# A fixed order for VectorE's first block, and one batch's sums on TensorE, in an attention and feed-forward kernel

## The chip, the cores and the metric

The kernel runs on one core of a Trainium2 chip. The metric is the device time of one execution in microseconds; the time before is the median of three runs.

## What is computed

Eight batches of 576 positions go through attention with eight heads of 64, whose keys and values are first averaged over groups of eight positions (72 per batch remain). The result, 4608 tokens of width 512, goes through two feed-forward layers. Reference, cut to what matters:

```python
k_p = k.reshape(B, H, Sp, 8, D).mean(axis=3)          # Sp = 72
v_p = v.reshape(B, H, Sp, 8, D).mean(axis=3)
scores = q @ k_p.transpose(0, 1, 3, 2) / sqrt(D)
attn = softmax(scores)                                 # max subtracted, 1e-9 added to the sum
x = (attn @ v_p)  -> rows of 512                       # 4608 x 512
h = x @ w_in;  g = h * sigmoid(1.702 * h);  x = g @ w_out        # 512 -> 2048 -> 512
out = ((x @ w_a) * (x @ w_b)) @ w_out2                 # 512 -> 1536 -> 512
```

The weights arrive as 64-bit floats.

## The kernel before

**Tiles and passes.** Tokens go in nine blocks of 512, each made of four *units* of 128. Each feed-forward layer is done in two passes over the nine blocks, with a part of its hidden columns each (six and ten tiles of 128 columns in layer 1, four and eight in layer 2). A *step* is one hidden tile f of one block: `emit_h` (L325) makes h = x w_in for 128 hidden columns with twelve matmuls into PSUM, then g; `emit_y` (L342) adds g's product with w_out into four accumulators, twelve matmuls more. Every operand is a pair of a high part in a rounded format and a low part that holds the rest, so each product is three matmuls (`mm3`, L110): high by high (L111), high by low (L112), low by high (L113). `split` (L68) makes such a pair: ScalarE rounds (L70), VectorE subtracts (L71).

**Weights.** A weight tile arrives as pairs of 32-bit words. `convert` (L87) makes high and low part out of them: four steps on VectorE (L92, L93, L94, L98), the rounding on ScalarE (L101), four more on VectorE (L103, L104, L107, L108). Each hidden tile has two such conversions, e = 0 for w_in and e = 1 for w_out.

**Attention.** `sum_k` (L165) adds groups of eight positions of the keys, half a batch's heads at a time, in one VectorE reduction (L170), and ScalarE copies the result in two pieces into `kbd` (L172, L173), laid out so that one matmul makes the scores of two heads. `sum_v` (L181) does the same for the values (L184). Per unit: `stage_b1` (L186), twice for four heads each, makes the scores on TensorE (L200), takes their maximum on VectorE (L207), scales and negates it (L208), and lets ScalarE take the exponentials with their sum (L211); `stage_b2` (L220) normalises on VectorE in three dependent steps (L223, L224, L225); `stage_c` (L227) transposes on TensorE (L233) and copies (L234); `stage_d` (L237) multiplies by the summed values (L246) and splits the result into x, high and low.

**What sets the order.** The program's text is followed by a list scheduler: it takes instructions by their place in the text and by modelled times, and interleaves independent work on each engine. What comes out is fixed: each engine works through its own queue in order and waits in front of an instruction until its operands are there. The exception before is `tc.issue_after(...)`, which holds later conversions behind a named instruction (`spread_late`, L421). At the start the text loads keys, queries, values and weights of batches 0 and 1 through SP's queue (L508 to L525), where each transfer waits for the one eight places ahead of it; does units 0 to 3 with the first weight tiles in between (L526 to L541); and then runs the steps, in each of which the text has the next step's `emit_h`, the extra work that `todo` holds (conversions, sums and attention of later units), and this step's `emit_y` (L552 to L562).

Of the kernel before, what the change touches and what calls it, by code (L numbers as in the profile page):

```python
# [24 lines left out]
def tile_kernel(ctx, tc, q, k, v, w_in, w_out, w_a, w_b, w_o2, out):  # L25
# [39 lines left out]
    def f32(ap):  # L65
        return ap.bitcast(F32)

    def split(hi, lo, src):  # L68

        nc.scalar.copy(out=hi, in_=src)  # L70
        nc.vector.tensor_tensor(out=lo, in0=src, in1=f32(hi), op=ALU.subtract)  # L71


    words = {
# [12 lines left out]
    def convert(units):  # L87


        for raw, t, hi, lo in units:  # L90
            low, high = raw[:, :, 0], raw[:, :, 1]
            nc.vector.tensor_scalar(out=t, in0=high, scalar1=0x7FFFFFFF, scalar2=None, op0=ALU.bitwise_and)  # L92
# [5 lines left out]
            nc.vector.scalar_tensor_tensor(  # L98
                out=t, in0=high, scalar=0xC0000000, in1=t, op0=ALU.bitwise_and, op1=ALU.bitwise_or
            )  # L100
            nc.scalar.copy(out=hi, in_=f32(t))  # L101

            nc.vector.tensor_scalar(out=high, in0=t, scalar1=0xFF800000, scalar2=None, op0=ALU.bitwise_and)  # L103
            nc.vector.scalar_tensor_tensor(  # L104
                out=f32(low), in0=low, scalar=2.0 ** -52, in1=f32(high), op0=ALU.mult, op1=ALU.mult
            )
            nc.vector.tensor_tensor(out=f32(t), in0=f32(t), in1=f32(hi), op=ALU.subtract)  # L107
            nc.vector.tensor_tensor(out=lo, in0=f32(t), in1=f32(low), op=ALU.add)  # L108

    def mm3(o, whi, wlo, xhi, xlo, first, last):  # L110
        nc.tensor.matmul(out=o, lhsT=whi, rhs=xhi, start=first, stop=False)  # L111
# [50 lines left out]
        nc.sync.dma_start(out=raw, in_=k[b, :, 2 * half:2 * half + 2, :])  # L162
        kraw_t[b, half] = raw

    def sum_k(b, half):  # L165
# [4 lines left out]
        nc.vector.tensor_reduce(out=ks, in_=raw, op=ALU.add, axis=AX.X)  # L170
        cs = slice(2 * half, 2 * half + 2)
        nc.scalar.copy(out=kbd[b % 2][0:D, cs, 0:SP], in_=ks[0:D])  # L172
        nc.scalar.copy(out=kbd[b % 2][D:P, cs, SP:2 * SP], in_=ks[D:P])  # L173
# [7 lines left out]
    def sum_v(b, h, n):  # L181
        if h == 0:
            vs_t[b] = ap_.tile([SP, H, D], F32, tag="vs", name="vs", bufs=2)
        nc.vector.tensor_reduce(out=vs_t[b][:, h:h + n, :], in_=vraw_t.pop((b, h)), op=ALU.add, axis=AX.X)  # L184

    def stage_b1(u, half):  # L186
        qT = q_t[u]
        if half == 0:
            at_t[u] = (
                ap_.tile([P, H, SP], F32, tag="at", name="at", bufs=2),  # L190
                ap_.tile([P, H], F32, tag="mx", name="mx", bufs=2),
                ap_.tile([P, H], F32, tag="sm", name="sm", bufs=2),
            )
        a, mx, sm = at_t[u]
        scale = 1.0 / (POOL * D ** 0.5)
# [12 lines left out]
        nc.vector.tensor_scalar_mul(mx[:, hs], mx[:, hs], -scale)  # L208
        for c in range(H // 2):
            h = half * (H // 2) + c  # L210
            nc.scalar.activation(  # L211
                out=a[:, h, :], in_=sc[:, c, :], func=AF.Exp, scale=scale, bias=mx[:, h:h + 1],
                accum_out=sm[:, h:h + 1],
            )
        if half == 1:
            q_t.pop(u)
            if UB <= u + 2 < NU:
                load_q(u + 2)

# [38 lines left out]
    def op(f, *a):  # L258
        return lambda: f(*a)
# [30 lines left out]
    def as_words(t):  # L290
        return t.rearrange("p (f w) -> p f w", w=2)
# [6 lines left out]
            return columns("a", f), columns("b", f)  # L298
        return rows("o2", 2 * f), rows("o2", 2 * f + 1)

    def load_w(key, raw=None):
        if raw is None:
            raw = wp.tile([P, 2, 1024], U32, tag="w", name="raw")
        raw_t[key] = raw
        for e, src in enumerate(sources(key)):
            nc.sync.dma_start(out=as_words(raw[:, e]), in_=src)

    nconv = [0]

    def make_w(key, e):  # L310

        if e == 0:
            w_t[key] = wp.tile([P, 4, 512], F32R, tag="w", name="w")
        w = w_t[key]
        t = tmps[nconv[0] % len(tmps)]
        nconv[0] += 1
        convert([(as_words(raw_t[key][:, e]), t, w[:, e, :], w[:, 2 + e, :])])
        if e == 1:
            raw_t.pop(key)


    anchors = {}
# [2 lines left out]
    def emit_h(i, j, f):  # L325
        xhi, xlo = x_t[i, j]
        w = w_t[1, f]
        hps = ps.tile([P, N], F32, tag="ps", name="h")
        for kk in range(KD):
            cs = slice(kk * P, (kk + 1) * P)  # L330
            mm3(hps, w[:, 0, cs], w[:, 2, cs], xhi[:, kk, :], xlo[:, kk, :], kk == 0, kk == KD - 1)

        g = gp.tile([P, N], F32, tag="g", name="g", bufs=1)
        ghi = gp.tile([P, N], F32R, tag="ghi", name="ghi")
        glo = gp.tile([P, N], F32R, tag="glo", name="glo")
        nc.scalar.activation(out=g, in_=hps, func=AF.Tanh, scale=0.5 * 1.702)  # L336
        made = nc.vector.scalar_tensor_tensor(out=g, in0=g, scalar=1.0, in1=hps, op0=ALU.add, op1=ALU.mult)  # L337
        split(ghi, glo, g)
        anchors[i, j, f] = made.ins
        g_t[i, j, f] = (ghi, glo)  # L340
# [187 lines left out]
    for t, ops in enumerate(slots):  # L528
        if t == 2:
            for half in range(2):  # L530
                sum_v(0, half * H // 2, H // 2)
        for o in ops:
            o()
        if t == 0:
            make_w((1, 0), 0)
        if t == 2:
            make_w((1, 0), 1)
            load_w((1, 3))
        if t == 3:
            make_w((1, 1), 0)  # L540
    make_w((1, 1), 1)  # L541

    for n in range(FA - 2):
        ops = [op(make_w, (1, n + 2), e) for e in range(2)]
        if n + 4 < FA:
            ops.append(op(load_w, (1, n + 4)))
        if n == 0:
            ops += [op(sum_k, 1, 0), op(sum_k, 1, 1), op(sum_v, 1, 0, H // 2), op(sum_v, 1, H // 2, H // 2)]
        todo[n] = ops + todo[n]

    first(steps[0])
    for n, s in enumerate(steps):  # L552
        if n == place[1, 0, FA]:
            at.close()
            p2 = ctx.enter_context(tc.tile_pool(name="p2", bufs=2))
            rooms += [p2.tile([P, 2, 1024], U32, name=f"room{e}", bufs=1) for e in range(2)]
            tmps[:] = [p2.tile([P, 512], U32, name=f"tmp{e}", bufs=1) for e in range(2)]
        if n + 1 < len(steps):
            first(steps[n + 1])
        for o in todo[n]:  # L560
            o()
        second(s)  # L562
# [47 lines left out]
```

## Time and profile before

| | |
|---|---|
| median of three runs | 1853.39 us (1850.32 to 1856.36) |
| the profiled execution | 1854.09 us |
| its span, first to last instruction | 1852.3 us |
| TensorE busy | 1803.3 us, 97% of the span, 8592 matmul records |
| VectorE busy | 847.4 us, 46% |
| ScalarE busy | 543.8 us, 29% |
| mean granted clock of TensorE | 0.987 |

In the profile PE is TensorE, DVE VectorE, ACT ScalarE and SP the engine that issues the transfers. The shares are means over the whole span and hide that its start is another regime than the rest; the windows below show the busy time of each engine by stretch. The granted clock is the share of TensorE's full 2.4 GHz that it ran at; 0.50 is its lower level of 1.2 GHz. A float32 matmul of the program (scores, transposed products) shows as two records, a transpose or a matmul of the rounded format as one. Consecutive rows of VectorE overlap a little: an instruction that does not depend on the one ahead starts before that one's end.

### The profile page before, as it was taken

How to read it: one execution, taken by the hardware profiler on the slowest of the kernel's cores; microseconds unless marked ns; L12 is line 12 of the kernel's file. 1: busy time of each engine (PE TensorE's matmuls, PEld its weight loads, DVE VectorE, ACT ScalarE, POOL GpSimd, SP SyncE). 2: the span in 40 equal slices, each digit the busy share in tenths (PEclk: the TensorE clock that was granted, in tenths of full speed). 3: DMA queues.
4: the chain of work that ended last, by engine and by line, in shares of the span. 5: the costliest groups of instructions: out<-in, count | busy, mean ns of one | idle time of the engine just before them, and what ended most of it. 6: DMA issues, size and time to landing. Idle time of an engine off the chain costs nothing.

```text
span 1852.3 us, 21637 instructions
## 1 busy us (share of the span) xinstructions
PE 1803.3 (97%) x8592; PEld 1485.8 (80%) x8592; DVE 847.4 (46%) x1524; ACT 543.8 (29%) x1361; POOL 1.7 (0%) x8
## 2 busy tenths in 40 slices
PE   3889999999999999999999999999999999999998
PEld 2668888888888888888888888888888888888887
DVE  7967677756644444445444444456212221221222
ACT  3556555554232222223222222222111111111111
POOL 0000000000000000000000000000000000000000
PEclk8789999999999999999999999999999999999999
DMA  8454444324433222333224433432201210220200
GB/s 259 163 180 150 165 148 157 127 86 163 178 114 110 96 100 93 126 125 134 100 82 152 159 137 105 168 114 91 91 28 64 91 61 30 91 91 8 84 24 23
DMA packets 58613, 206.92 MB, mean 112 GB/s; under 512 B 6576, under 2 KB 6576, under 8 KB 46704
## 3 DMA queue, kind: packets, MB, share of 16 engines
q1 hardware_dynamic: 58512, 205.55, 31.4%
q8 instruction: 67, 1.10, 0.2%
q14 instruction: 34, 0.28, 0.1%
HBM read 139.46 MB, written 66.06 MB: 111 GB/s over the span
## 4 chain that ended last, share of the span: by engine, by line
PE 94%; DMA 3%; DVE 2%; ACT 0%; issue 0%; SPq 0%; DVEq 0%; ACTq 0%
PE ab L112 11%; PE ab L111 11%; PE ab L113 11%; PE acc L112 7%; PE acc L111 7%; PE acc L113 7%; PE h L111 7%; PE h L112 7%; PE h L113 7%; PE acc L376 5%; PE acc L375 5%; PE acc L377 5%; PE sc L200 2%; PE px L246 2%; PE pt L233 2%; DMA kraw<-in_k_dram 1%
## 5 line engine op out<-in xcount | busy, mean ns | idle before, releaser
L111 PE MATMUL ab<-xhi,w 128*128 128x512 f32 x864 | 336.1, 389 | 0.0
L112 PE MATMUL ab<-xlo,w 128*128 128x512 f32 x864 | 336.1, 389 | 0.0
L113 PE MATMUL ab<-xhi,w 128*128 128x512 f32 x864 | 336.1, 389 | 0.0
L363 DVE TENSOR_TENSOR c<-c,ab 128x512 f32<-128x512 f32 x108 | 74.2, 687 | 530.3 <-PE ab L113 530.3
L112 PE MATMUL acc<-glo,w 128*128 128x512 f32 x576 | 229.0, 398 | 5.0 <-DVE glo L71 5.0
L113 PE MATMUL acc<-ghi,w 128*128 128x512 f32 x576 | 227.6, 395 | 0.0
L111 PE MATMUL h<-xhi,w 128*128 128x512 f32 x576 | 226.2, 394 | 0.7 <-ACT xhi L70 0.7
L112 PE MATMUL h<-xlo,w 128*128 128x512 f32 x576 | 224.9, 390 | 0.0
L113 PE MATMUL h<-xhi,w 128*128 128x512 f32 x576 | 224.6, 390 | 0.0
L337 DVE SCALAR_TENSOR_TENSOR g<-g,h 128x512 f32<-128x512 f32 x144 | 98.5, 684 | 228.4 <-ACT g L336 228.0
L111 PE MATMUL acc<-ghi,w 128*128 128x512 f32 x576 | 187.6, 401 | 3.9 <-ACT ghi L70 3.8
L111 PEld LDWEIGHTS ab<-xhi,w 128*128 128x128 f32 x864 | 162.2, 188 | 33.8
L113 PEld LDWEIGHTS ab<-xhi,w 128*128 128x128 f32 x864 | 162.2, 188 | 33.7
L112 PEld LDWEIGHTS ab<-xlo,w 128*128 128x128 f32 x864 | 162.2, 188 | 33.6
L336 ACT ACTIVATE g<-h 128x512 f32<-128x512 f32 x144 | 86.1, 598 | 322.5 <-PE h L113 309.8
L376 PE MATMUL acc<-w,chi 128*128 128x512 f32 x432 | 168.1, 389 | 0.0
L375 PE MATMUL acc<-w,chi 128*128 128x512 f32 x432 | 168.1, 389 | 0.0
L362 ACT COPY c<-ab 128x512 f32<-128x512 f32 x108 | 63.4, 587 | 356.3 <-PE ab L113 356.3
L377 PE MATMUL acc<-w,clo 128*128 128x512 f32 x432 | 167.6, 389 | 0.0
L70 ACT CAST chi<-c 128x512 fp32r<-128x512 f32 x108 | 66.9, 620 | 288.4 <-DVE c L363 288.4
L112 PEld LDWEIGHTS acc<-glo,w 128*128 128x128 f32 x576 | 109.3, 190 | 28.4 <-DVE glo L71 6.2
L111 PEld LDWEIGHTS acc<-ghi,w 128*128 128x128 f32 x576 | 107.4, 190 | 26.5 <-ACT ghi L70 5.1
(61 smaller groups left out, 2070.8 us busy)
## 6 DMA issues: line engine op xcount, KB each, us to landing
part<-ys SPq DMA_DIRECT2D x72, 256.0 KB
part<-part SPq DMA_DIRECT2D x18, 1024.0 KB
xhi<-yd SPq DMA_DIRECT2D x18, 1024.0 KB
xlo<-yd SPq DMA_DIRECT2D x18, 1024.0 KB
xd<-xhi SPq DMA_DIRECT2D x9, 1024.0 KB
xd<-xlo SPq DMA_DIRECT2D x9, 1024.0 KB
xhi<-xd SPq DMA_DIRECT2D x9, 1024.0 KB
xlo<-xd SPq DMA_DIRECT2D x9, 1024.0 KB
```

Source lines behind the costliest of these rows:

```text
L70: nc.scalar.copy(out=hi, in_=src)
L111: nc.tensor.matmul(out=o, lhsT=whi, rhs=xhi, start=first, stop=False)
L112: nc.tensor.matmul(out=o, lhsT=whi, rhs=xlo, start=False, stop=False)
L113: nc.tensor.matmul(out=o, lhsT=wlo, rhs=xhi, start=False, stop=last)
L200: nc.tensor.matmul(out=sc[o:o + n, 2 * c:2 * c + 2, :].rearrange("p h k -> p (h k)"), lhsT=qT[:, pair, o:o + n], rhs=kbd[b % 2][:, pair, : ...
L336: nc.scalar.activation(out=g, in_=hps, func=AF.Tanh, scale=0.5 * 1.702)
L337: made = nc.vector.scalar_tensor_tensor(out=g, in0=g, scalar=1.0, in1=hps, op0=ALU.add, op1=ALU.mult)
L362: nc.scalar.copy(out=cc, in_=pab[0])
L363: made = nc.vector.tensor_tensor(out=cc, in0=cc, in1=pab[1], op=ALU.mult)
L375: nc.tensor.matmul(out=o, lhsT=chi[:, cs], rhs=whi, start=first, stop=False)
L376: nc.tensor.matmul(out=o, lhsT=chi[:, cs], rhs=wlo, start=False, stop=False)
L377: nc.tensor.matmul(out=o, lhsT=clo[:, cs], rhs=whi, start=False, stop=last)
```

## The change

1. *A fixed order for VectorE in the first block.* `vec` notes the newest VectorE instruction of a group, and `in_order` issues each next group behind it, so that the groups stand in VectorE's queue in the order of the text. The work before the first step, and that beside the six steps of the first block, is written out in this way. A conversion is cut in two parts (`part` 0 and 1), `emit_h` gives back its two VectorE steps as pieces, and `filler` puts conversion parts and attention pieces between them.
2. *Batch 1's sums on TensorE.* `sum_k_pe` and `sum_v_pe` add the eight positions by eight matmuls with the identity into one PSUM tile, each reading every eighth word of the raw keys or values; ScalarE copies the sums out. Batches 0 and 2 to 7 keep the reductions.
3. *Scaling.* The keys are scaled when they are copied into `kbd`, the maximum is negated by the reduction that takes it, and the multiplication (L208) is gone.
4. *The first conversion step* of the six tiles of the first pass is an absolute value on ScalarE instead of a mask on VectorE.
5. *Loads.* Part e = 1 of the first weight tile is loaded behind the values of batch 0 and the second unit's queries.

```diff
+    def in_order(*ops):
+        for o in ops:
+            if newest[0] is None:
+                o()
+            else:
+                with tc.issue_after(newest[0]):
+                    o()
...
+            if first_on_act:
+                nc.scalar.activation(out=f32(t), in_=f32(high), func=AF.Abs)
+            else:
+                nc.vector.tensor_scalar(out=t, in0=high, scalar1=0x7FFFFFFF, scalar2=None, op0=ALU.bitwise_and)
...
+    def to_kbd(b, half, ks):
+        cs = slice(2 * half, 2 * half + 2)
+        nc.scalar.mul(out=kbd[b % 2][0:D, cs, 0:SP], in_=ks[0:D], mul=scale)
+        nc.scalar.mul(out=kbd[b % 2][D:P, cs, SP:2 * SP], in_=ks[D:P], mul=scale)
...
+    def sum_k_pe(b, half):
+        ks = ps.tile([P, 2, SP], F32, tag="ps", name="ksp")
+        raw = kraw_t.pop((b, half)).rearrange("p c (s r) -> p c s r", r=POOL)
+        for r in range(POOL):
+            nc.tensor.matmul(out=ks, lhsT=ident, rhs=raw[:, :, :, r], start=r == 0, stop=r == POOL - 1)
+        to_kbd(b, half, ks)
...
+    def sum_v_pe(b, h, n):
...
+        vp = ps.tile([SP, n, D], F32, tag="ps", name="vsp")
+        for r in range(POOL):
+            nc.tensor.matmul(
+                out=vp, lhsT=ident[:SP, :SP], rhs=raw[:, :, :, r], start=r == 0, stop=r == POOL - 1
+            )
+        nc.scalar.copy(out=vs_t[b][:, h:h + n, :], in_=vp)
...
-        nc.vector.tensor_reduce(out=mx[:, hs], in_=sc, op=ALU.max, axis=AX.X)
-        nc.vector.tensor_scalar_mul(mx[:, hs], mx[:, hs], -scale)
+        vec(nc.vector.tensor_reduce(out=mx[:, hs], in_=sc, op=ALU.max, axis=AX.X, negate=True))
...
+    c0, c1 = make_parts((1, 0)), make_parts((1, 1))
+    in_order(op(sum_k, 0, 0), op(sum_k, 0, 1), b1(0)[0], c0[0], b1(0)[1], b1(1)[0], c0[1], b1(1)[1])
+    in_order(op(sum_v, 0, 0, half_v), b2(0), op(sum_v, 0, half_v, half_v), b2(1), *b1(2))
+    in_order(c0[2], cd(0), b1(3)[0], c0[3], cd(1), b1(3)[1], b2(2), c1[0], b2(3), c1[1], cd(2), c1[2], cd(3), c1[3])
...
+    hs[0] = emit_h(*steps[0])
     for half in range(2):
-        sum_k(0, half)
...
+        sum_k_pe(1, half)
+    in_order(hs[0][0])
+    filler(1)
+    in_order(hs[0][1])
+    for n in range(1, FA):
+        hs[n] = emit_h(*steps[n])
+        second(steps[n - 1])
+        if n == 1:
+            sum_v_pe(1, 0, half_v)
+            sum_v_pe(1, half_v, half_v)
+        filler(2)
+        in_order(hs[n][0])
+        filler(1)
+        in_order(hs[n][1])
+        filler(1)
+    in_order(*ahead_)
```

VectorE's queue before, from the first g (L337) on: `tmp_126` and `tmp_127` are two conversions in work, `raw_298` and `raw_469` their tiles, `mx` the maxima, `ks` a key sum.

```order
L337 SCALAR_TENSOR_TENSOR g_423<-g_423,h_410 128x512
L103 TENSOR_SCALAR raw_298<-tmp_127 128x512
L92 TENSOR_SCALAR tmp_126<-raw_469 128x512
L207 TENSOR_REDUCE mx_484<-sc_497 128x4
L170 TENSOR_REDUCE ks_979<-kraw_892 128x144
L207 TENSOR_REDUCE mx_513<-sc_515 128x4
L104 SCALAR_TENSOR_TENSOR raw_298<-raw_298 128x512
L107 TENSOR_TENSOR tmp_127<-tmp_127,w_593 128x512
L93 TENSOR_SCALAR tmp_126<-tmp_126 128x512
L207 TENSOR_REDUCE mx_513<-sc_527 128x4
L71 TENSOR_TENSOR glo_425<-g_423,ghi_424 128x512
```

The same place of the changed kernel, whose first g is L395, g's low half L400, the first conversion half L111 to L116, the second L122 to L127, and a unit's normalisation L266 to L268:

```order
L111 TENSOR_SCALAR tmp_126<-tmp_126 128x512
L112 TENSOR_SCALAR tmp_126<-tmp_126 128x512
L116 SCALAR_TENSOR_TENSOR tmp_126<-raw_151,tmp_126 128x512
L251 TENSOR_REDUCE mx_453<-sc_455 128x4
L251 TENSOR_REDUCE mx_453<-sc_465 128x4
L400 TENSOR_TENSOR glo_417<-g_415,ghi_416 128x512
L122 TENSOR_SCALAR raw_151<-tmp_126 128x512
L123 SCALAR_TENSOR_TENSOR raw_151<-raw_151 128x512
L126 TENSOR_TENSOR tmp_126<-tmp_126,w_446 128x512
L127 TENSOR_TENSOR w_446<-tmp_126,raw_151 128x512
L251 TENSOR_REDUCE mx_539<-sc_541 128x4
L266 TENSOR_SCALAR sm_454<-sm_454 128x8
```

Two conversions were interleaved step by step with sums and maxima; now the steps of one half follow each other, and the maxima of units 4 and 5 stand between the halves.

TensorE's queue before, at the first activation (`h_410`; `h_430` is the second, `sc` scores of unit 4, `kbd0` and `kbd1` the keys of batches 0 and 1):

```order
L111 MATMUL h_410<-xhi_252,w_187 128x512
L111 MATMUL h_430<-xhi_252,w_351 128x512
L200 MATMUL sc_486<-kbd0_122,q_274 64x144
L200 MATMUL sc_486<-kbd1_123,q_274 64x144
L200 MATMUL sc_486<-kbd0_122,q_274 64x144
L200 MATMUL sc_486<-kbd1_123,q_274 64x144
L112 MATMUL h_410<-xlo_253,w_187 128x512
```

The same place of the changed kernel, with the first activation `h_402` and the key sums `ksp` by halves of the heads:

```order
L130 MATMUL h_402<-xhi_265,w_180 128x512
L205 MATMUL ksp_419<-kvraw_147,ident_78 128x144 x8
L205 MATMUL ksp_430<-kvraw_149,ident_78 128x144 x2
L131 MATMUL h_402<-xlo_266,w_180 128x512
L132 MATMUL h_402<-xhi_265,w_180 128x512
L130 MATMUL h_402<-xhi_265,w_180 128x512
```

Ten of the sixteen key-sum matmuls now stand inside the first activation; the other six follow it, then unit 4's scores.

## Rows read from the trace of the kernel before

**Rows 1.** Busy time of each engine (instructions) by windows; granted clock; DMA share, GB/s.

```profile
0.00:30.00 30.00, 8.62 (x36) 6.95 (x36) 21.30 (x39) 11.20 (x45) 1.73 (x8) 1.00 0.96 296
30.00:60.00 30.00, 17.39 (x102) 12.81 (x102) 25.86 (x52) 13.19 (x46) 0.00 (x0) 0.57 0.52 161
60.00:100.00 40.00, 32.94 (x184) 25.09 (x180) 38.50 (x83) 20.50 (x80) 0.00 (x0) 0.84 0.57 192
100.00:120.00 20.00, 17.79 (x87) 14.07 (x88) 11.91 (x24) 10.95 (x45) 0.00 (x0) 0.76 0.31 90
120.00:1852.00 1732.00, 1726.59 (x8191) 1426.84 (x8189) 749.84 (x1329) 487.94 (x1147) 0.00 (x0) 1.00 0.30 106
```

**Rows 2.** Who waited for whom, 0 to 130 us: total us, times, longest.

```profile
PE pt L233 <- DVE at L225: 19.7, 4, 8.5
...
PE acc L112 <- DVE glo L71: 5.0, 2, 3.3
...
DVE ks L170 <- ACT kbd L173: 2.0, 1, 2.0
```

**Rows 3.** VectorE's timeline, a later conversion and a normalisation: start us, us.

```profile
1028.28 0.69 DVE L98 SCALAR_TENSOR_TENSOR tmp<-room,tmp 128x512 uint32<-128x512 uint32 x1
1029.01 0.43 DVE L103 TENSOR_SCALAR room<-tmp 128x512 uint32<-128x512 uint32 x1
1029.47 0.69 DVE L104 SCALAR_TENSOR_TENSOR room<-room 128x512 f32<-128x512 uint32 x1
1030.08 0.68 DVE L107 TENSOR_TENSOR tmp<-tmp,w 128x512 f32<-128x512 f32 x1
1030.80 0.69 DVE L108 TENSOR_TENSOR w<-tmp,room 128x512 fp32r<-128x512 f32 x1
...
105.75 0.17 DVE L223 TENSOR_SCALAR sm<-sm 128x8 f32<-128x8 f32 x1 [0.79 <-ACT at L211]
105.96 0.20 DVE L224 RECIPROCAL sm<-sm 128x8 f32<-128x8 f32 x1
106.20 0.76 DVE L225 TENSOR_TENSOR at<-at,sm 128x576 f32<-128x576 f32 x1
```

**Rows 4.** VectorE's timeline where conversions are interleaved, 64 to 66 us.

```profile
64.63 0.41 DVE L94 TENSOR_SCALAR tmp<-tmp 128x512 uint32<-128x512 uint32 x1
64.97 0.68 DVE L104 SCALAR_TENSOR_TENSOR raw<-raw 128x512 f32<-128x512 uint32 x1
65.57 0.68 DVE L107 TENSOR_TENSOR tmp<-tmp,w 128x512 f32<-128x512 f32 x1
```

**Rows 5.** Groups by line, 0 to 130 us: busy us, mean ns, idle before.

```profile
L184 DVE TENSOR_REDUCE vs<-kvraw 72x256 f32<-72x2048 f32 x4 | 9.1, 2280 | 3.3 <-DMA kvraw<-in_v_dram 3.2
L207 DVE TENSOR_REDUCE mx<-sc 128x4 f32<-128x288 f32 x20 | 8.9, 446 | 4.4 <-PE sc L200 4.3
...
L170 DVE TENSOR_REDUCE ks<-kvraw 128x144 f32<-128x1152 f32 x4 | 5.4, 1350 | 7.7 <-DMA kvraw<-in_k_dram 5.7 <-ACT kbd L173 2.0
...
L184 DVE TENSOR_REDUCE vs<-vraw 72x128 f32<-72x1024 f32 x4 | 4.8, 1211 | 2.5 <-DMA vraw<-in_v_dram 2.5
...
L208 DVE TENSOR_SCALAR mx<-mx 128x4 f32<-128x4 f32 x20 | 3.0, 156 | 0.0
...
L101 ACT CAST w<-tmp 128x512 fp32r<-128x512 f32 x12 | 7.5, 626 | 21.1 <-DVE tmp L98 21.1
```

**Rows 6.** TensorE's timeline: scores at both clocks, end of the second block's first activation.

```profile
39.41 1.17 PE L200 MATMUL sc<-kbd,qs 128*128 128x144 f32 x4
...
84.43 0.65 PE L200 MATMUL sc<-kbd,q 128*128 128x144 f32 x4
84.83 0.49 PE L112 MATMUL acc<-glo,w 128*128 128x512 f32 x1
...
128.93 0.39 PE L112 MATMUL h<-xlo,w 128*128 128x512 f32 x1
129.16 0.39 PE L113 MATMUL h<-xhi,w 128*128 128x512 f32 x1
```

More of the change, by code (lines that the diff above doesn't have):

```diff
@@ L85, in rows, with convert @@
         return words[name][f * P:(f + 1) * P, :, :]
[L87 to L92, printed above, removed]
+    def convert(raw, t, hi, lo, part, first_on_act=False):
+        low, high = raw[:, :, 0], raw[:, :, 1]
+        if part == 0:
+            if first_on_act:
+                nc.scalar.activation(out=f32(t), in_=f32(high), func=AF.Abs)
+            else:
+                nc.vector.tensor_scalar(out=t, in0=high, scalar1=0x7FFFFFFF, scalar2=None, op0=ALU.bitwise_and)
             nc.vector.tensor_scalar(out=f32(t), in0=f32(t), scalar1=LOW, scalar2=HIGH, op0=ALU.max, op1=ALU.min)
@@ L96, in convert @@
             )
-            nc.vector.scalar_tensor_tensor(
+            vec(nc.vector.scalar_tensor_tensor(
                 out=t, in0=high, scalar=0xC0000000, in1=t, op0=ALU.bitwise_and, op1=ALU.bitwise_or
-            )
+            ))
             nc.scalar.copy(out=hi, in_=f32(t))
[L103 to L108, printed above, removed]
+            return
+        nc.vector.tensor_scalar(out=high, in0=t, scalar1=0xFF800000, scalar2=None, op0=ALU.bitwise_and)
+        nc.vector.scalar_tensor_tensor(
+            out=f32(low), in0=low, scalar=2.0 ** -52, in1=f32(high), op0=ALU.mult, op1=ALU.mult
+        )
+        nc.vector.tensor_tensor(out=f32(t), in0=f32(t), in1=f32(hi), op=ALU.subtract)
+        vec(nc.vector.tensor_tensor(out=lo, in0=f32(t), in1=f32(low), op=ALU.add))
     def mm3(o, whi, wlo, xhi, xlo, first, last):
@@ L169, in sum_k @@
         raw = kraw_t.pop((b, half)).rearrange("p c (s r) -> p c s r", r=POOL)
[L170 to L173, printed above, removed]
+        vec(nc.vector.tensor_reduce(out=ks, in_=raw, op=ALU.add, axis=AX.X))
+        to_kbd(b, half, ks)
[4 more added lines that the diff above has]
+            nc.tensor.matmul(out=ks, lhsT=ident, rhs=raw[:, :, :, r], start=r == 0, stop=r == POOL - 1)
+        to_kbd(b, half, ks)
     def load_v(b, h, n, raw=None):
@@ L211, in stage_b1 @@
             nc.scalar.activation(
-                out=a[:, h, :], in_=sc[:, c, :], func=AF.Exp, scale=scale, bias=mx[:, h:h + 1],
+                out=a[:, h, :], in_=sc[:, c, :], func=AF.Exp, bias=mx[:, h:h + 1],
                 accum_out=sm[:, h:h + 1],
@@ L299, in sources, with load_w @@
         return rows("o2", 2 * f), rows("o2", 2 * f + 1)
-    def load_w(key, raw=None):
+    def load_w(key, raw=None, parts=(0, 1)):
         if raw is None:
@@ L305, in load_w @@
         for e, src in enumerate(sources(key)):
+            if e not in parts:
+                continue
             nc.sync.dma_start(out=as_words(raw[:, e]), in_=src)
@@ L316, in make_w, with make_parts, one @@
         nconv[0] += 1
-        convert([(as_words(raw_t[key][:, e]), t, w[:, e, :], w[:, 2 + e, :])])
+        for part in range(2):
+            convert(as_words(raw_t[key][:, e]), t, w[:, e, :], w[:, 2 + e, :], part)
         if e == 1:
             raw_t.pop(key)
+    def make_parts(key):
+        def one(e, part):
+            if (e, part) == (0, 0):
+                w_t[key] = wp.tile([P, 4, 512], F32R, tag="w", name="w")
+            w = w_t[key]
+            convert(as_words(raw_t[key][:, e]), tmps[e], w[:, e, :], w[:, 2 + e, :], part, True)
+        return [op(one, e, part) for e in range(2) for part in range(2)]
     anchors = {}
@@ L336, in emit_h, with rest @@
         nc.scalar.activation(out=g, in_=hps, func=AF.Tanh, scale=0.5 * 1.702)
[L337 to L340, printed above, removed]
+        def rest():
+            made = vec(nc.vector.scalar_tensor_tensor(out=g, in0=g, scalar=1.0, in1=hps, op0=ALU.add, op1=ALU.mult))
+            nc.scalar.copy(out=ghi, in_=g)
+            anchors[i, j, f] = made.ins
+            g_t[i, j, f] = (ghi, glo)
+        return rest, lambda: vec(nc.vector.tensor_tensor(out=glo, in0=g, in1=f32(ghi), op=ALU.subtract))
     def emit_y(f, gs, ya, first, last):
@@ L433, in first @@
         i, j, f = s
-        (emit_h if passes[i][0] == 1 else emit_ab)(i, j, f)
+        if passes[i][0] == 1:
+            for o in emit_h(i, j, f):
+                o()
+        else:
+            emit_ab(i, j, f)
     sums = {}
@@ L445, in second @@
             finish(i, j, sums.pop((i, j)))
-    for j in range(1, NB):
-        ts = range(UB if j == 1 else UB * j + 2, UB * (j + 1) + 2)
-        spread([o for t in ts for o in later[t]], max(0, place[0, j - 1, 0] - 1), place[0, j, 0] - 1)
+    for j in range(2, NB):
+        ts = range(UB * j + 2, UB * (j + 1) + 2)
+        spread([o for t in ts for o in later[t]], place[0, j - 1, 0] - 1, place[0, j, 0] - 1)
     for i in range(1, 4):
@@ L513, in tile_kernel @@
     next(kv0)
-    load_w((1, 0))
-    next(kv0)
+    load_w((1, 0), parts=(0,))
     load_q(1, qs[:, 1])
     next(kv0)
+    next(kv0)
+    load_w((1, 0), raw_t[1, 0], (1,))
     load_q(2, qs[:, 2])
+    load_q(3, qs[:, 3])
     load_w((1, 1))
-    load_q(3, qs[:, 3])
     next(kv1)
@@ L525, in tile_kernel @@
     next(kv1)
-    for half in range(2):
-        sum_k(0, half)
[L528 to L549, printed above, removed]
@@ L551, in tile_kernel, with b1, b2, cd @@
-    first(steps[0])
+    load_w((1, 3))
+    half_v = H // 2
+    def b1(u):
+        return [op(stage_b1, u, half) for half in range(2)]
+    def b2(u):
+        return op(stage_b2, u)
+    def cd(u):
+        return lambda: (stage_c(u), stage_d(u))
+    c0, c1 = make_parts((1, 0)), make_parts((1, 1))
+    in_order(op(sum_k, 0, 0), op(sum_k, 0, 1), b1(0)[0], c0[0], b1(0)[1], b1(1)[0], c0[1], b1(1)[1])
+    in_order(op(sum_v, 0, 0, half_v), b2(0), op(sum_v, 0, half_v, half_v), b2(1), *b1(2))
+    in_order(c0[2], cd(0), b1(3)[0], c0[3], cd(1), b1(3)[1], b2(2), c1[0], b2(3), c1[1], cd(2), c1[2], cd(3), c1[3])
@@ new lines, in tile_kernel, with filler @@
+    ahead_ = [o for t in range(UB, 2 * UB + 2) for o in later[t]]
+    parts = [o for f in range(2, FA) for o in make_parts((1, f))]
+    per = -(-len(ahead_) // len(parts))
+    hs = {}
+    def filler(n):
+        for _ in range(n):
+            if parts:
+                f = FA - len(parts) // 4
+                if len(parts) % 4 == 0 and f + 2 < FA:
+                    load_w((1, f + 2))
+                in_order(parts.pop(0))
+            in_order(*ahead_[:per])
+            del ahead_[:per]
```

18 lines of the change are left out of this document (14 added, 4 removed).

## The prediction

> **What bounds the kernel now.** I read the windows first, then who TensorE waits for, then VectorE's rows. The windows show that the kernel is TensorE from 120 us on: 1726.6 us busy in 1732 us at a granted clock of 1.00 [rows 1]. What a change can win lies before that. In the first 120 us TensorE is busy 8.6 + 17.4 + 32.9 + 17.8 = 76.7 us, so it idles 43.3 us, and part of the rest runs at a granted clock of 0.57 to 0.84, a mixture of its levels of 1.2 and 2.4 GHz. VectorE is busy 38.5 of 40 us between 60 and 100 us in the same stretch. The waits [rows 2] say the same from the other side: TensorE stands 19.7 us for the normalised attention weights and 5.0 us for the low half of g, both VectorE's. So the head is VectorE's, and the sum has to be made along its queue. DMA is full only in the first 30 us, with 296 GB/s.
>
> I measure both kernels at one place: where TensorE has done the first block of 512 tokens and the first activation of the second. Before, the last matmul of that activation starts at 129.16 us [rows 6] and lasts to 129.4, the next instruction's start. Everything behind it is full TensorE in both, so what is gained there is gained at the end.
>
> **The change, part by part.** VectorE loses: two key sums and two value sums of the second batch, which go to TensorE (2 x 1.27 + 2 x 2.20 = 6.9 us; rows of 1.35 and 2.28 us [rows 5], of which the next instruction overlaps 0.08); the first step of twelve weight conversions, which goes to ScalarE (12 x 0.34 = 4.0 us at the dense spacing of [rows 4]); twenty small multiplications of the maximum (0.156 us each [rows 5], less the same overlap: 1.5 us). Together 12.4 us.
>
> VectorE gains a price through the order. Where an instruction needs nothing of the one in front, starts follow 0.34 us (64.63 to 64.97) and 0.60 us (64.97 to 65.57) apart, shorter than the rows themselves [rows 4]. Where it needs the result, it waits for the end: 0.73 us from 1028.28 to 1029.01, 0.46 to 1029.47, 0.72 from 1030.08 to 1030.80, and 0.61 where it doesn't [rows 3]. The list scheduler of before put other work between dependent steps; the new lists keep a conversion half and a normalisation together, as the pieces of order show. A conversion costs 0.46 + 0.46 + 0.60 for its first half and 0.46 + 0.61 + 0.72 + 0.60 for its second, 3.9 us, where the remaining seven steps packed cost 3 x 0.34 + 4 x 0.60 = 3.4. A normalisation costs 0.21 + 0.24 + 0.67 = 1.12 us from starts and busy time [rows 3], where it packs into about 0.85. Over eleven conversions and ten normalisations that is 5.3 + 2.7 = 8.0 us given back.
>
> The Trainium skill weighs this otherwise: VectorE: DVE Perf Modes, "The DRAIN you can't avoid", says that eight copies take the same time with a semaphore after each or only after the last. By that the 8.0 us would not be there. The trace does not agree: 0.34 against 0.46 for the same operation. I keep the rows.
>
> VectorE's queue in the new order, up to the second weight half that the sixth activation needs: eleven conversions 42.9; ten normalisations 11.2; twenty maxima at 0.37, 7.4; five key sums 6.3; two large and four small value sums 4.4 + 4.5 (each by its mean row less 0.08 [rows 5]); eight x splits, four g and four low halves of g at 0.60, 9.6. Sum 86.3 us. It starts at 5.0 us, with the first key data, as before.
>
> To that come the waits, found by walking the new order of all three engines with the same durations. (1) 2.1 us for the key copies, as before [rows 2], and 0.8 for ScalarE's new first step; that step is one more pass over 128x512, at the 0.626 us of a cast [rows 5]. ScalarE does twelve, 7.5 us, beside 21.1 us that it idled for this work. (2) Four short waits on x of units 0 to 3, 3.5 us together. x is then complete at about 41 us, against 60. (3) First g: TensorE runs one matmul of h, ten of the sixteen key-sum matmuls and the other eleven of h; VectorE is back from its conversion at 43.8, g can start at about 49: 5.0 us. (4) The maximum of unit 4's second half stands behind the other key sums, the second activation and four output matmuls: 2.8 us. (5) The maximum of unit 5 stands behind the sixteen value-sum matmuls and the low half of the outputs: 4.6 us. Sum 18.8.
>
> The sums on TensorE are the unknown price. A program matmul of 144 columns is two records; four records start within 0.40 us at 84.43, and four take 1.17 us at 39.41 at the low clock [rows 6]. So a record is 0.10 to 0.28 us, and of 256 columns, by the ratio, 0.18 to 0.49. Thirty-two of each are 8.9 to 24.5 us. I take 4.4 us for the first twenty (clock still low for most), 1.3 for the next twelve and 5.8 for the value sums at the high clock, 11.5 us in all, nearer the low end, because TensorE has no pause from 41 us on. They lie on VectorE's path through waits (3) to (5), so nothing hides them.
>
> 5.0 + 86.3 + 18.8 = 110.1 us. Then TensorE has the sixth and seventh activation (24 matmuls at the 0.23 us of 128.93 to 129.16 [rows 6], 5.5 us) and, as before's order had them earlier, the outputs of blocks 4 and 5 (another 5.5). I add 1.2 us, since a key sum and two value sums (3.5 us) now stand ahead of the sixth g. 122.3 against 129.4: 7.1 us sooner. The profiled execution took 1854.09 us for a span of 1852.3; less 7.1 it is 1847.0. The median of the runs shown is 0.7 us below the profiled one: 1846.3, and I say 1846.5.
>
> Edits at nothing: keys scaled in the copy (the same two passes per half), the exponential without a scale, and the new order of loads. The second half of the first weights lands later, behind 1.4 MB that take 4.8 us at the 296 GB/s of [rows 1], so at some 17 us; its first use is at about 23. If it came later than that, the excess would be paid once, in full.
>
> **Rivals.**
> A. *The sums hold VectorE up* (slower). At 18.6 us for the sums instead of 11.5 the gain is gone; at the upper bound of 24.5 the end is 1846.5 + 13 = 1859.5. For it: the clock of 0.57 between 30 and 60 us, and that each new matmul reads every eighth word of its rows, which no row of before does. Against it: scores at 0.10 us a record as soon as TensorE is busy.
> The Trainium skill speaks for A: SBUF — State Buffer, under "Door 1: The DMA port swizzle", has lines of 16 bytes, with a penalty for each access that goes to a new one, and here every word is in a new one. A doubled read would give about A's time. No run so far shows it.
> B. *The clock takes it back* (no change). Between 64 and 73 us and again at 95 to 99, I find TensorE waiting for VectorE in pieces of one to four microseconds. If it falls to 1.2 GHz there, twenty matmuls cost 0.23 us more each, 4.6 us: 1851. For it: before fell to a mean of 0.76 after 100 us with such waits. Against: the pieces near 70 are short.
> C. *The waits of (3) to (5) close* (more gain). If the sums run at 0.10 and 0.18 from the start and the scores come in time, up to 12.4 us more: 1834. The dependent spacing at nothing would be 8.0 us more, 1838.5. For it: x is ready 19 us sooner. Against: TensorE's queue has the sums in front of the scores.
>
> **How the numbers follow.** Forecast 0.48 (1842 to 1851), A 0.14, B 0.24, C 0.14. The range 1836 to 1857 leaves out the far parts of A and C. 0.3%, what a measurement tells from no change, is 5.6 us: faster means below 1847.8, slower above 1859. Faster has two thirds of the forecast and all of C, 0.46; slower, most of A and what I haven't seen, 0.14; the rest, 0.40, is no change.
>
> **What would show it.** First g at about 49 us and x complete at about 41, against 67 and 60. Key and value sums of 11 to 12 us on TensorE; over 18 means A. VectorE's steps of a conversion 0.46 and 0.72 us apart. TensorE without gaps from about 110 us, at a clock of 1.00; a low clock at 70 to 80 means B. If first g is early but the sixth g not before 121 us, a later wait has taken the gain. Wrong altogether would be TensorE waiting behind 130 us.

## The result and the profile after

The changed kernel takes 1863.69 us (1862.61 to 1865.65, five runs) against 1850.32 for the kernel before on the same chip: a ratio of 1.0068, 95% interval 1.0047 to 1.0088. It is slower, by 13.4 us. Forecast were 1846.5, 6.9 below the 1853.39 that the forecast began from, and a range up to 1857. Two executions of the experiments below, of 4704.1 us in 5 and of 2044.5 us in 6, are left out of the medians there.

The profiled execution has a span of 1861.4 us, 9.1 more than before. VectorE is busy 836.5 us, 10.9 less; TensorE 1827.5, 24.2 more. The windows answer to [rows 1] (columns as there):

```profile
30.00:60.00 30.00, 26.77 (x129) 20.29 (x130) 16.43 (x33) 13.43 (x44) 0.00 (x0) 0.73 0.64 227
60.00:100.00 40.00, 36.76 (x171) 24.41 (x170) 23.87 (x47) 19.22 (x72) 0.00 (x0) 0.74 0.17 51
100.00:120.00 20.00, 14.23 (x79) 10.53 (x78) 17.60 (x34) 10.49 (x40) 0.00 (x0) 0.77 0.39 129
120.00:150.00 30.00, 29.37 (x147) 23.02 (x146) 24.64 (x39) 13.91 (x49) 0.00 (x0) 0.92 0.73 237
```

Between 60 and 100 us VectorE, which was full there before (38.5 of 40 us), is busy 23.9 us, and TensorE 36.8. The head of the kernel has changed its bound. Who waited for whom from 0 to 130 us (total us, times, longest), against [rows 2], names the place:

```profile
DVE mx L251 <- PE sc L244: 20.7, 4, 15.3
...
DVE g L395 <- ACT g L392: 6.2, 1, 6.2
PE pt L276 <- DVE at L268: 5.5, 3, 3.0
```

TensorE waits for normalised weights 5.5 us instead of 19.7, as was meant. In exchange VectorE waits 20.7 us for scores, 15.3 of them at once. In VectorE's timeline (start us, us, idle before it and what ended it) the three places are easily found; its first, sixth and last rows are the waits that the forecast calls (3), (4) and (5), and the fifth is the first maximum of unit 4:

```profile
50.22 0.69 DVE L395 SCALAR_TENSOR_TENSOR g<-g,h 128x512 f32<-128x512 f32 x1 [6.15 <-ACT g L392]
50.82 0.42 DVE L111 TENSOR_SCALAR tmp<-tmp 128x512 f32<-128x512 f32 x1
51.27 0.43 DVE L112 TENSOR_SCALAR tmp<-tmp 128x512 uint32<-128x512 uint32 x1
51.74 0.69 DVE L116 SCALAR_TENSOR_TENSOR tmp<-raw,tmp 128x512 uint32<-128x512 uint32 x1
53.37 0.46 DVE L251 TENSOR_REDUCE mx<-sc 128x4 f32<-128x288 f32 x1 [0.94 <-PE sc L244]
58.12 0.46 DVE L251 TENSOR_REDUCE mx<-sc 128x4 f32<-128x288 f32 x1 [4.30 <-PE sc L244]
...
76.88 0.46 DVE L251 TENSOR_REDUCE mx<-sc 128x4 f32<-128x288 f32 x1 [15.31 <-PE sc L244]
```

What TensorE did meanwhile stands in its timeline, which answers to [rows 6]. A program matmul of the sums is two records, so the key sums are 20 + 12 records of 144 columns and the value sums 24 + 8 of 256. How long a group lasts is read from the next row's start:

```profile
41.60 5.44 PE L205 MATMUL ksp<-kvraw,ident 128*128 128x144 f32 x20
46.65 0.63 PE L131 MATMUL h<-xlo,w 128*128 128x512 f32 x1
...
49.39 3.29 PE L205 MATMUL ksp<-kvraw,ident 128*128 128x144 f32 x12
52.61 0.95 PE L244 MATMUL sc<-kbd,q 128*64 128x144 f32 x10
...
58.01 11.26 PE L226 MATMUL vsp<-kvraw,ident 72*72 72x256 f32 x24
68.67 1.02 PE L131 MATMUL acc<-glo,w 128*128 128x512 f32 x1
...
72.48 3.87 PE L226 MATMUL vsp<-kvraw,ident 72*72 72x256 f32 x8
76.17 1.63 PE L244 MATMUL sc<-kbd,q 128*128 128x144 f32 x8
```

That is 5.05 + 3.22 + 10.66 + 3.69 = 22.6 us for the sums. Scores of the same 144 columns, ten records in 0.88 us at 52.61, take 0.09 us each, and a key-sum record just ahead of them, at the same clock, 0.27. (These scores are half as wide, 128*64 in their rows against 128*128; experiment 2 has the like comparison.) The long wait ends as soon as the scores behind the last sums are there.

The groups by line from 0 to 130 us (busy us, mean ns, idle before) answer to [rows 5]: the maxima cost what they did, the multiplications and four large sums are gone from VectorE, ScalarE's new first step lasts 0.67 us, and the rows of the sums on TensorE (15.1 + 8.7) make up nearly all of the 24 us that it has more.

```profile
L226 PE MATMUL vsp<-kvraw,ident 72*72 72x256 f32 x32 | 15.1, 641 | 0.0
...
L251 DVE TENSOR_REDUCE mx<-sc 128x4 f32<-128x288 f32 x20 | 8.8, 451 | 20.8 <-PE sc L244 20.7
L205 PE MATMUL ksp<-kvraw,ident 128*128 128x144 f32 x32 | 8.7, 441 | 0.0
...
L108 ACT ACTIVATE tmp<-raw 128x512 f32<-128x512 f32 x12 | 8.0, 666 | 8.8 <-DVE w L127 7.2 <-DMA raw<-in_moe_w_out_dram 0.8 <-DMA raw<-in_moe_w_in_dram 0.8
```

The clock is the third reading. In narrower windows of the same trace:

```profile
60.00:62.00 2.00, 2.00 (x6) 0.69 (x5) 1.54 (x3) 0.42 (x1) 0.00 (x0) 1.00 0.05 17
62.00:64.00 2.00, 2.00 (x5) 0.76 (x4) 0.00 (x0) 0.00 (x0) 0.00 (x0) 0.77 0.00 0
64.00:66.00 2.00, 2.00 (x6) 1.00 (x5) 0.00 (x0) 0.38 (x2) 0.00 (x0) 0.50 0.00 0
...
68.60:72.40 3.80, 3.80 (x10) 2.84 (x9) 0.00 (x0) 0.00 (x0) 0.00 (x0) 0.50 0.00 0
72.40:76.10 3.70, 3.70 (x9) 1.48 (x8) 0.00 (x0) 0.00 (x0) 0.00 (x0) 0.88 0.00 0
```

TensorE is listed as busy for the whole of each window, and yet the granted clock falls from 1.00 (2.4 GHz) to 0.50 (1.2 GHz) in the middle of the value sums. The sums don't mind: a record takes 0.44 us in the first group, half of which runs at 1.00 and half at 0.50, and 0.46 in the second, at 0.88. The eight outputs between them do: 3.8 us, where at the high clock they take 2.0 (below).

### The profile page after: what moved, and what is told of

It is laid out like the page before. It is cut to its first block, busy times and chain, and to the rows that moved or that the text cites. A ratio compares the mean times of both kernels' runs of the same rounds, so it can differ in the third digit from the quotient of the medians.

```text
span 1861.4 us, 21690 instructions
## 1 busy us (share of the span) xinstructions
PE 1827.5 (98%) x8656; PEld 1499.9 (81%) x8656; DVE 836.5 (45%) x1436; ACT 549.6 (30%) x1375; POOL 1.7 (0%) x8
## 4 chain that ended last, share of the span: by engine, by line
PE 96%; DVE 2%; DMA 1%; ACT 1%; issue 0%; DVEq 0%; ACTq 0%
PE ab L132 11%; PE ab L130 11%; PE ab L131 11%; PE acc L130 7%; PE acc L131 7%; PE acc L132 7%; PE h L130 7%; PE h L131 7%; PE h L132 7%; PE acc L435 5%; PE acc L436 5%; PE acc L437 5%; PE px L289 2%; PE sc L244 2%; PE pt L276 2%; PE vsp L226 1%
## 5 line engine op out<-in xcount | busy, mean ns | idle before, releaser
L395 DVE SCALAR_TENSOR_TENSOR g<-g,h 128x512 f32<-128x512 f32 x144 | 98.5, 684 | 236.7 <-ACT g L392 236.3
L130 PEld LDWEIGHTS h<-xhi,w 128*128 128x128 f32 x576 | 108.9, 189 | 24.1 <-ACT xhi L85 1.1
```

Of the source, the lines that this page charges most:

```text
L395: made = vec(nc.vector.scalar_tensor_tensor(out=g, in0=g, scalar=1.0, in1=hps, op0=ALU.add, op1=ALU.mult))
```

## Experiments

All times are medians of five or more runs (but for the single run behind the profile in 5), with the ratio to the kernel before on the same chip and its 95% interval. The theory that had to be tested: the sums' reading of every eighth word sets their pace (S). Its rivals: such matmuls with the identity are slow whatever they read, by their shape or by the two records of a float32 product (W); or the fixed order itself is what loses (F).

**1. Consecutive reads, wrong groups.** The same matmuls read eight runs of neighbouring words; so batch 1's keys and values are added in other groups than the reference's.

```diff
-        raw = kraw_t.pop((b, half)).rearrange("p c (s r) -> p c s r", r=POOL)
+        raw = kraw_t.pop((b, half)).rearrange("p c s -> p (c s)").rearrange("p (r c s) -> p r c s", r=POOL, c=2)
...
-            nc.tensor.matmul(out=ks, lhsT=ident, rhs=raw[:, :, :, r], start=r == 0, stop=r == POOL - 1)
+            nc.tensor.matmul(out=ks, lhsT=ident, rhs=raw[:, r], start=r == 0, stop=r == POOL - 1)
```

> The changed kernel, its sums on TensorE reading consecutive words instead of every eighth (batch 1's groups are then other positions, so the sums are of the wrong groups; counts and shapes are the same). Theory S, the stride sets the pace of the sums: records of 144 columns at about 0.10 us on a full clock (0.25 to 0.27 now), of 256 columns at about 0.18 (0.46 now), 22.6 us become 9 to 11, and the time falls by about 12 to 1851. Rival W, the two-pass products or the 72-wide shape are slow by themselves: records stay at 0.25 and 0.46 us and the time at 1863.

Measured: 1852.56 us, ratio 1.0009 (1.0000 to 1.0018). Some 11 us are gone, and only the reads were changed.

**2. Consecutive reads, right groups.** The same edit, and batch 1's keys and values are laid out in memory with the position within its group as the slow index, so that the computation is the reference's.

```diff
+            a[1] = a[1].reshape(s // POOL, 2, h // 2, d, POOL).transpose(0, 1, 4, 2, 3).reshape(a[1].shape)
```

> The changed kernel with batch 1's keys and values laid out in memory with the position in the group ahead of the rest, so that the same sums read consecutive words; the computation is the reference's. Theory S: as with consecutive words of wrong groups, about 1851, so the change without its stride is no slower than before. Rival W: 1863.

Measured: 1851.52 us, ratio 1.0005 (0.9996 to 1.0015). TensorE's timeline, at the places shown above for the changed kernel:

```profile
50.27 1.63 PE L205 MATMUL ksp<-kvraw,ident 128*128 128x144 f32 x12
51.83 0.95 PE L244 MATMUL sc<-kbd,q 128*64 128x144 f32 x10
...
57.19 5.40 PE L226 MATMUL vsp<-kvraw,ident 72*72 72x256 f32 x24
62.24 0.59 PE L131 MATMUL acc<-glo,w 128*128 128x512 f32 x1
...
64.27 1.89 PE L226 MATMUL vsp<-kvraw,ident 72*72 72x256 f32 x8
66.00 1.15 PE L244 MATMUL sc<-kbd,q 128*128 128x144 f32 x8
```

Twelve key records take 1.56 us instead of 3.22, 24 value records 5.05 instead of 10.66, eight 1.73 instead of 3.69; the eight outputs from 62.24 take 2.03. Same shapes, same identity, same two records: W falls. The first twenty key records, which run mostly at the low clock, take 4.63 against 5.05, so there the stride costs little. All sums: 13.0 instead of 22.6 us, 9.6 less; the time falls by 12.2, and the 1.8 us of the outputs are most of the rest.

**3. The fixed order without the sums.** Batch 1's sums stay on VectorE, in the fixed order.

```diff
-    for half in range(2):
-        sum_k_pe(1, half)
+    in_order(op(sum_k, 1, 0), op(sum_k, 1, 1))
...
-            sum_v_pe(1, 0, half_v)
-            sum_v_pe(1, half_v, half_v)
+            in_order(op(sum_v, 1, 0, half_v), op(sum_v, 1, half_v, half_v))
```

> The changed kernel with batch 1's sums back on VectorE, in the fixed order. If the sums on TensorE are what costs (theory S or W alike): 22.6 us leave TensorE, 6.9 come to VectorE of which 2.5 fill its wait for the first g, so about 16 us less, 1846 to 1849. Rival F, the fixed order itself is the loss (no other work between dependent steps): stays at 1860 or above.

Measured: 1845.56 us, ratio 0.9968 (0.9957 to 0.9980), just below the range expected. F falls: the change's other parts, together, make the kernel faster. VectorE's timeline at the place of waits (3) and (4):

```profile
45.06 1.35 DVE L197 TENSOR_REDUCE ks<-kvraw 128x144 f32<-128x1152 f32 x1
47.19 1.35 DVE L197 TENSOR_REDUCE ks<-kvraw 128x144 f32<-128x1152 f32 x1 [0.78 <-ACT kbd L192]
49.41 0.69 DVE L395 SCALAR_TENSOR_TENSOR g<-g,h 128x512 f32<-128x512 f32 x1 [0.87 <-ACT g L392]
...
52.18 0.95 DVE L251 TENSOR_REDUCE mx<-sc 128x4 f32<-128x288 f32 x2 [0.55 <-PE sc L244]
...
53.64 4.47 DVE L217 TENSOR_REDUCE vs<-kvraw 72x256 f32<-72x2048 f32 x2
```

The key sums lie in time in which VectorE would otherwise wait for the first h. The books can be kept with these waits. Here VectorE waits 0.78 + 0.87 + 0.55 = 2.2 us at the three places, in the changed kernel 6.15 + 0.94 (unit 4's first maximum) + 4.30 + 15.31 = 26.7. It has 6.9 us less to do there. 26.7 - 2.2 - 6.9 = 17.6 us, and the two times differ by 18.1. With the consecutive reads of experiment 2 VectorE's waits are these:

```profile
51.09 0.69 DVE L395 SCALAR_TENSOR_TENSOR g<-g,h 128x512 f32<-128x512 f32 x1 [5.76 <-ACT g L392]
...
57.30 0.46 DVE L251 TENSOR_REDUCE mx<-sc 128x4 f32<-128x288 f32 x1 [3.62 <-PE sc L244]
...
66.69 0.46 DVE L251 TENSOR_REDUCE mx<-sc 128x4 f32<-128x288 f32 x1 [5.94 <-PE sc L244]
```

They sum to 15.3, so 15.3 - 2.2 - 6.9 = 6.2, and the times differ by 6.0. So even at full pace the move loses 6 us: TensorE's 13.0 us lie in front of the first h and the scores for which VectorE waits.

**4. The sums alone.** The kernel before, its order untouched, with batch 1's sums on TensorE, read with the stride.

```diff
-            ops += [op(sum_k, 1, 0), op(sum_k, 1, 1), op(sum_v, 1, 0, H // 2), op(sum_v, 1, H // 2, H // 2)]
+            ops += [op(sum_k_pe, 1, 0), op(sum_k_pe, 1, 1), op(sum_v_pe, 1, 0, H // 2), op(sum_v_pe, 1, H // 2, H // 2)]
```

> The kernel before, with only batch 1's sums moved to TensorE, every eighth word as in the change. Theory S or W: 20 us and more of sums stand in TensorE's queue at 60 us ahead of unit 4's scores, VectorE saves 6.9; slower by 5 to 13, 1855 to 1863. Rival F: the move alone costs nothing, 1848 to 1852.

Measured: 1854.12 us, ratio 1.0027 (1.0017 to 1.0036). That is 3.4 us above the 1850.73 of the kernel before beside it: the move costs time by itself, though less than the 5 to 13 us expected. The windows show the same sight as above, TensorE busy without a gap at a falling clock:

```profile
60.00:80.00 20.00, 20.00 (x61) 10.73 (x60) 9.39 (x18) 3.66 (x9) 0.00 (x0) 0.61 0.01 2
```

The move costs 0.27% in the old order and about 1% in the new one (1.0068 against 0.9968). In both VectorE comes to a long wait for scores, 9.9 us here and 15.3 there; a likely reason for the difference, not tried by itself, is that in the fixed order the maximum of unit 5 stands ahead of all that could have been done meanwhile.

**5. Keys or values.** The changed kernel with only the values laid out for consecutive reads. Theory V has the values' reading alone lower the clock, theory K the keys' as well. The profile is that of a further run.

> The changed kernel with only batch 1's values laid out for consecutive reads; the keys are read with the stride as before. Strided key sums took 8.3 us of TensorE against 6.2, strided value sums 14.4 against 6.7, so the sums should take 8.3 + 6.7 = 15.0 us. Theory V (the value sums' reading alone set off the low clock): key records 0.25 to 0.27 us, value records 0.21, the clock 1.00 from 57 to 80 us, and 1863.7 less 7.7 for the sums less 2 to 3 for the clock: 1853.5 us (1852.5 to 1855). Theory K (the strided key sums lower the clock as well, and the value sums start at 0.50): 1856 to 1858 us, with scores and outputs at twice their time behind 60 us.

> The same kernel as the run with only the values laid out for consecutive reads, which took 1855.2 us, for its rows. Theory V (the value sums' reading alone set off the low clock): key records 0.25 to 0.27 us apart, value records 0.21, the clock 1.00 from 57 to 70 us. Theory K (the strided key sums lower it as well): the clock at 0.50 behind the key sums, scores and outputs at twice their time before 65 us.

Measured: 1855.0 us, ratio 1.0024 (1.0014 to 1.0034); the further run took 1856.33. Records (shortest, median, longest ns) by tile, and a window, of that run:

```profile
L205 PE MATMUL ksp<-kvraw,ident x32: 419/440/449, 42.7 to 53.5; 128*128 128x144 f32 x32
...
L226 PE MATMUL vsp<-kvraw,ident x32: 377/379/437, 59.3 to 67.9; 72*72 72x256 f32 x32
```

```profile
63.00:66.00 3.00, 3.00 (x15) 2.27 (x14) 0.00 (x0) 0.93 (x2) 0.00 (x0) 1.00 0.00 0
```

Strided key records last 440 ns as in the changed kernel, consecutive value records 379 instead of 640, and the clock stays at 1.00 where it fell: theory V, and the time is the upper end of V's range. Of the 12.2 us that the stride costs, 8.7 go with the values and 3.5 with the keys, each difference uncertain by some 2 us.

**6. Is it the length of the sums that lowers the clock?** The kernel of experiment 2 with each value sum made twice, the second over the first.

```diff
-        for r in range(POOL):
+        for r in list(range(POOL)) * 2:
```

> The kernel with batch 1's keys and values laid out for consecutive reads (1851.5 us), with the value sums made twice: the eight matmuls per half run, and run again over the first result, 32 records of 256 columns more. It asks why the clock fell to 0.50 in the middle of the strided value sums, though TensorE had no gap there. Theory L (length: a long stretch of such matmuls with the identity lowers the clock, however it reads): records stay near 0.21 us, the sums last about 13 us, and the clock falls to 0.50 some 5 us into them and stays low behind them; about 1861 us. Theory P (pace: it is the slow reading, in which TensorE is counted busy and mostly waits, that lowers the clock): the clock stays at 1.00 from 55 to 80 us, and the time rises by the records alone, 32 x 0.21 = 6.7 us, to about 1858 us (1856.5 to 1859.5). If the time hardly rises (under 1853), the value sums are not on the path that sets the end.

Measured: 1857.7 us, ratio 1.0041 (1.0026 to 1.0057). The windows:

```profile
60.00:65.00 5.00, 5.00 (x25) 3.50 (x24) 0.00 (x0) 0.37 (x1) 0.00 (x0) 1.00 0.00 0
65.00:70.00 5.00, 5.00 (x25) 3.33 (x24) 0.00 (x0) 0.00 (x0) 0.00 (x0) 1.00 0.00 0
70.00:75.00 5.00, 3.15 (x22) 2.44 (x20) 4.09 (x9) 3.95 (x20) 0.00 (x0) 0.95 0.21 52
75.00:80.00 5.00, 4.94 (x41) 3.99 (x41) 4.86 (x11) 3.86 (x14) 0.00 (x0) 0.50 0.46 132
```

The clock is 1.00 to the end of the sums at 70 us, 16 us after their start at 54.4, where the strided ones had lost it some 5 us after theirs at 58.0. It falls only behind a stretch with gaps (3.15 us busy of 5.00 from 70 us on). The 6.2 us more (6.7 by the ratios) fit the 32 records, 32 x 0.21 = 6.7. So theory P is borne out and L is not: with the slow reading the clock falls, though the records show no gap, and without it the same sums, even twice as many, leave it up.

**7. Two conversions side by side.** The kernel of experiment 3, in which the two conversions of a tile are made step beside step from the second tile on, to test the price of dependent steps. The pieces of conversion that the fixed order puts between the other work are then half as many and twice as long.

```diff
-    parts = [o for f in range(2, FA) for o in make_parts((1, f))]
+    parts = [o for f in range(2, FA) for o in make_pairs((1, f))]
...
+            for _ in zip_longest(*[
+                steps_of(as_words(raw_t[key][:, e]), tmps[e], w[:, e, :], w[:, 2 + e, :], part, True) for e in range(2)
+            ]):
+                pass
```

> The version with the fixed order and batch 1's sums on VectorE (1845.6 us), with the two conversions of a weight tile made together, step beside step, from the second tile on (five tiles), so that fewer steps stand directly behind the step they need. Theory D (dependent steps cost what the rows of before say): a first half falls from 2 x (0.46 + 0.46 + 0.60) = 3.04 us to 4 x 0.34 + 2 x 0.60 = 2.56, a second from 4.78 to about 4.3; 1.0 us for each of five tiles, 4.9 us on VectorE, of which some goes into waits: 1841 to 1844 us. Rival Q (what VectorE saves it waits for, or a longer piece ahead of g and of g's low half holds TensorE): rows 0.34 us apart, and 1845 us or more.

Measured: 1841.85 us, ratio 0.9955 (0.9942 to 0.9968), the fastest version of all. VectorE's timeline, two first halves together:

```profile
47.77 0.76 DVE L117 TENSOR_SCALAR tmp<-tmp 128x512 f32<-128x512 f32 x2
48.44 0.75 DVE L119 TENSOR_SCALAR tmp<-tmp 128x512 uint32<-128x512 uint32 x2
49.11 1.29 DVE L124 SCALAR_TENSOR_TENSOR tmp<-raw,tmp 128x512 uint32<-128x512 uint32 x2
50.32 1.18 DVE L263 TENSOR_REDUCE mx<-sc 128x4 f32<-128x288 f32 x3
```

They take 50.32 - 47.77 = 2.55 us, forecast 2.56; in the changed kernel one takes 1.52 (0.45 + 0.47 from start to start and the 0.60 of a dense step), two 3.04. Theory D holds for the price of the steps. The time is in D's range too, but against the kernel of experiment 3 it is lower by only 0.13% by the ratios, some 2.4 us, with intervals that overlap; so the gain isn't told apart from none, and the longer pieces may have a share in it.

**8. The mask back on VectorE.** The kernel of experiment 3 with the first step of the conversions where it was before.

```diff
-            convert(as_words(raw_t[key][:, e]), tmps[e], w[:, e, :], w[:, 2 + e, :], part, True)
+            convert(as_words(raw_t[key][:, e]), tmps[e], w[:, e, :], w[:, 2 + e, :], part)
```

> The version with the fixed order and batch 1's sums on VectorE (1845.6 us), with the first step of the twelve conversions put back from ScalarE to VectorE. Twelve steps of 0.46 us at the dependent spacing are 5.5 us; of that about 0.8 us of waiting for ScalarE's first pass goes. If VectorE's queue is what the head of the kernel waits for, 1849.5 to 1851 us, all of the fixed order's gain. If VectorE's idle 3.9 us between 60 and 100 us take it up, 1846 to 1847.5 us.

Measured: 1847.04 us, ratio 0.9980 (0.9970 to 0.9989). The step on ScalarE is worth 1.5 us by the medians and 2.2 by the ratios, not the 4.0 us of VectorE's time that it removes (5.5 at the dependent spacing). This is the second range expected, in which VectorE's idle time takes the rest up; but from 60 to 100 us that time shrinks only from 3.9 to 3.2 us, so where the rest goes isn't shown. The intervals of the two experiments overlap.

## Why the prediction was wrong

**The step that failed** is the price of the sums on TensorE, "11.5 us in all, nearer the low end, because TensorE has no pause from 41 us on". For its three terms of 4.4, 1.3 and 5.8 us the trace has 5.05, 3.22 and 14.35: 22.6 us. The bounds, 8.9 to 24.5, held it. The choice between them rested on scores, which take half the time at the high clock; a matmul that reads every eighth word does not. With consecutive reads the sums take 13.0 us, 1.5 above the forecast; the other 9.6 are the stride, which the sum left out. That is rival A, given 0.14, with its deciding point of 18.6 us passed.

**Waits (3) to (5)** carry it. The first g is at 50.2 (forecast 49), the second maximum of unit 4 at 58.1 and the first of unit 5 at 76.9. From the forecast's terms the two maxima come out at about 54.3 (49 + 0.60 + 1.52 + 0.37 + 2.8) and 62.3 (54.3 + 0.37 + 0.60 + 2.39 + 4.6). Of the 14.6 us between 62.3 and 76.9, 11.1 are the sums, 1.8 the outputs at the low clock, and 1.7 are left over.

**The clock** was expected to stay up "because TensorE has no pause from 41 us on". It had none, and fell to 0.50 all the same. By A's own rule 22.6 us of sums would give 1846.5 + 11.1 = 1857.6; the 1.8 us that the clock cost at the outputs and the smaller misses ahead of them and behind took the result past A's upper end of 1859.5.

**What held.** x is complete at 41.6 us (41); the steps of a conversion follow 0.45 and 0.47 us apart, the dependent price; from the maximum of unit 5 to the second weight half of the sixth activation VectorE needs 50.0 us, where the forecast had 110.1 - 62.3 = 47.8. It is done at 126.9, 16.8 late. (Two slips in the forecast are too small to matter: 12 x 0.34 is 4.1 and not 4.0, and [rows 2] have 2.0 us for the key copies and not 2.1.) Behind that the forecast's point doesn't exist as it was drawn, since TensorE's order is another: the seventh activation, the second block's first, ends at 132.7, ahead of the last outputs of the first block, which end at 145.1 with an eighth activation among them.

```profile
132.49 0.40 PE L132 MATMUL h<-xhi,w 128*128 128x512 f32 x1
...
144.84 0.39 PE L132 MATMUL acc<-ghi,w 128*128 128x512 f32 x1
```

An estimate of the like point is 129.4 + 9.1 = 138.5, from the difference of the two spans and with TensorE taken as equally full behind it. That is 11.6 us behind 126.9, where 12.2 were forecast, and 16.2 behind 122.3.

Scaling and the order of the loads, costed at nothing, were not tried by themselves. With the sums taken out, the forecast's sum would be 110.1 + 6.9 for the sums back on VectorE - 12.4 for waits (3) to (5) + the 2.2 of experiment 3 = 106.8 and 12.2 behind it, 10.4 us before 129.4; the kernel of experiment 3 gained 5.9 by its ratio (0.0032 x 1850), the right sign and not the size. By these terms the move would have lost, even with sums of 11.5 us, 110.1 - 106.8 = 3.3 us; the forecast never set the change beside one without it.

**Rivals B and C.** The clock did take time back, and B's sign, a low clock at 70 us, came; but it fell during the sums, not behind gaps. C didn't come: with the sums on TensorE none of the waits closed, with consecutive reads neither.

The Trainium skill, SBUF — State Buffer, under "Door 1: The DMA port swizzle", says that accesses within one 16-byte line run at full bandwidth and each step to a new line pays. These runs agree that scattered words are slower: 0.44 to 0.46 us against 0.21 a record of 256 columns, 0.27 against 0.13 of 144 at the high clock. Only words 32 bytes apart and neighbouring ones were run, so they do not show that 16 bytes are the limit. In the forecast I named this section and gave it no weight in the sum, since no row of before had such a read.

## What to carry to other kernels

Moving a sum to TensorE by identity matmuls is priced by its reads: look at the distance between the words that one column after the other takes, and if no row shows such a distance, choose the upper bound or lay the data out first. Count what the receiving engine has queued behind the work: 6.9 us taken off VectorE came back as 13.1 us (consecutive reads) to 24.5 us (strided) more of waiting for the first h and the scores that stood behind it. And work that fills an idle stretch is free where it is: with the key sums in front of the first g, VectorE still waited 0.87 us for it.

## What the runs showed of the hardware

- A float32 matmul whose moving operand takes one word in every 32 bytes lasts about 1.8 ns a column and record (10.66 us / 24 / 256 and 3.22 / 12 / 144 = 1.7 and 1.9), at a granted clock of 1.00, 0.88 and 0.50 alike; with consecutive words 0.8 and 0.9 at 1.00 (5.05 / 24 / 256 and 1.56 / 12 / 144). Mostly at the low clock the consecutive ones take 1.6 (4.63 / 20 / 144), so there the distance costs little.
- TensorE's granted clock can fall to 0.50 while its rows show no gap. The Trainium skill, TensorE: Matmul & The Clock Gate, under "What's actually happening", has the clock follow how busy TensorE was. Busy time as the rows list it does not agree (2.00 us busy of 2.00, clock 0.50). What TensorE did before the fall was the strided value sums; the same sums with consecutive reads, made twice, left the clock at 1.00. How the chip counts was not measured.
